# Opening of a fused attention and gated-FFN kernel on one core: weight loads on a second queue, reordered token loads, clearings on other engines, split first products

## The chip, the cores and the metric

The kernel runs on one core of a Trainium2 chip. The metric is device time of one execution in microseconds (us); lower is better. The kernel before has a median of 558.58 us in 3 runs (558.48 to 558.62).

## The reference

One block of a transformer over 2048 tokens of width 576, in bf16:

```
xn = layernorm(x)                                   # x: 2048 x 576
q, k, v = split(xn @ wqkv)                          # 32 heads of width 18
p = softmax(q k^T / sqrt(18)), causal, window 256
s = (p v) @ wo
h = sigmoid(xn @ w_gate) * (xn @ w_up)              # width 4608
g = silu(h @ w_down)
out = x + s * g
```

## The kernel before, in words

The tokens are worked off in four chunks of 512. For each chunk the kernel normalises four tiles of 128 tokens, brings them into the transposed form `xn` (features on the partitions), makes twelve projections (q, k and v for four tiles each), then runs the gate and up products (L910) with the score products (L697) and the products with v (L754) strewn among them, the output projection (L824) and the down projection (L1057, L1088, L1112). TensorE (PE) works with two 64-row halves side by side, so that nearly every product is a pair of matmuls that run together.

Nothing of the order is left to the hardware. Python objects of class `Op` carry an engine, a planned duration, dependencies and a priority; `schedule` (L1158) places them one after the other on five engine lists by planned times, `emit` (L1301) writes the lists out with semaphore waits. Each engine then works its list strictly in order. `deps` become waits on the chip, `odeps` and `behind` only set the order in the plan. The priority counts 40 ns a step, lower first; `slack` is added to the planned arrival of a DMA. So a change of a priority, a slack or a planned duration can move instructions anywhere in the program.

The change is about the first twenty microseconds, chunk 0:

- `build_init` (L367) clears and fills buffers. `pre` fills a tile of ones on VectorE (DVE), `warm` (L394) runs `WARM` = 10 products of 512 columns on it on PE. The identity for the transposes (`id1`, `id2`), masks (`m1`, `m2`, `m3`) and the ones in the v buffer (`vones`, `vpad`) are made on GpSimd (POOL), `hm` on DVE. `pkz` and three `ez` pieces zero the buffers for q and k on ScalarE (ACT): `pkz` the one for tile 0, `ez0` to `ez2` those for tiles 1 to 3.
- `build_ln` (L445) loads a tile of x (`x0` to `x3`, 128 x 576 each, L457), takes the statistics on DVE in two halves (`bn1` L461, `bn2` L463) and joins them (`ag` L465), computes the inverse deviation on POOL (`rstd` L468), applies both on DVE (`apply` L472) and copies 64 columns for the wrap-around (`wrap` L476). In chunk 0 PE transposes the tile in two groups, 8 matmuls that need `apply` and 10 that also need `wrap` (L498), and ACT copies each group from PSUM into `xn` (`xe` L510).
- `build_weights` (L414) loads wqkv: for each of q, k and v four pieces (`load9`, L403), pieces 0 and 3 of 64 x 5 x 288 and pieces 1 and 2 of 64 x 4 x 288.
- `project` (L517) makes one projection: 9 steps of two matmuls (64 rows, 288 columns, L524). For the q products of the tiles named in `Q_SPLIT` it is cut in two: a first part of 8 matmuls, which needs pieces 0 and 1 of the q weights and the first `xe`, and a second of 10, which needs the rest. `build_qk` (L568) brings the result from PSUM into the q and k buffer on ACT and DVE (L586).

In the program before, the DMA queue of SyncE (SP) issues x0, x1, x2, x3, then the four q pieces, four v pieces, four k pieces, then the gate and up weights. ACT issues no DMA. PE's order in the opening is: warm-up, transposes of tiles 0 and 1, first part of q0, transposes of tile 2, first part of q1, second part of q0, transposes of tile 3, second part of q1, then the other products without a break.

Of the kernel before, what the change touches and what calls it, by code (L numbers as in the profile page):

```python
# [8 lines left out]
D = 576  # L9
H = 32  # L10
DH = 18
F = 4608
P = 128
CH = 512
NCH = S // CH
QPC = CH // P
# [8 lines left out]
DP = NKT * P  # L25
# [16 lines left out]
NOT = 4  # L42
# [58 lines left out]
LATE_SLACK = 5000.0  # L101
LN_STEP = 1
EZ = 2
XT_CUT = 4
Q_SPLIT = (0, 1)
# [4 lines left out]
WARM = 10  # L110
X0_SLACK = -250.0
QKV_SLACK = 300.0
X_PRIO = (-9, -9, -9, -9)
# [4 lines left out]
X0_FACTOR = 1.7  # L118
# [100 lines left out]
class Builder:  # L219
# [46 lines left out]
    def alloc_memory(self):  # L266
        nc = self.nc
        bf16, f32 = dt.bfloat16, dt.float32
# [41 lines left out]
        self.pkf = self.pk.bitcast(f32)  # L310
        self.far = self.hT[:, FAR:FAR + 7, :].rearrange("p t c -> p (t c)")[:, 0:NC * FG * P].rearrange(
# [55 lines left out]
    def build_init(self):  # L367
        op = self.op
        self.op_negh = op("DVE", 60, lambda e: e.memset(self.neghalf[:, :], -0.5), "neghalf", prio=0)
        ep = op("POOL", 60, lambda e: e.memset(self.bnst[:, :, 12:14], 0.0), "eps0", prio=-5)  # L370
        self.op_eps = op("POOL", 60, lambda e: e.memset(self.bnst[:, :, 14:15], EPS * D), "eps1", deps=[ep], prio=-5)
        self.op_pre = op("DVE", 250, lambda e: e.memset(self.hT[:, 0, :], 1.0), "pre", prio=-9)
# [11 lines left out]
        h0 = op("DVE", 70, lambda e: e.memset(self.hm[:, :], 0.0), "hm", prio=0)  # L384
        self.op_hm = [op("DVE", 70, lambda e, q=q: e.memset(self.hm[32 * q:32 * q + 32, q % 2:q % 2 + 1], 1.0),
                         f"hm:{q}", deps=[h0], prio=0) for q in range(4)]
        vo1 = op("POOL", 1100, lambda e: e.memset(self.vau[:, :, :, 0:H // 2, DH:DH + 1], 1.0), "vones", prio=1, odeps=[m1])
        self.op_vones = op("POOL", 300, lambda e: e.memset(self.vau[:, :, :, H // 2, :], 1.0), "vpad", deps=[vo1], prio=1)
        self.warm(WARM, "warm:0", [self.op_pre])
        self.op_pkz = [op("ACT", 1300 + 950, lambda e: e.memzero(self.pk[:, 0:2, :, :]), "pkz", prio=0)]  # L390
        self.op_ez = [op("ACT", 930, lambda e, k=k: e.memzero(self.expr[:, 2 * k:2 * k + 2, :, :]), f"ez{k}", prio=0)
                      for k in range(QPC - 1)]
# [21 lines left out]
    def build_weights(self):  # L414
        wq = self.wqkv
        self.op_wqkv = [None] * 3
        for j in range(3):
# [27 lines left out]
    def build_ln(self, c):  # L445
        op = self.op
        pr = 0 if c == 0 else 2
        _, dxn = self.r_xn.take()
        self.op_xn = [[] for _ in range(QPC)]
        for i in range(QPC):  # L450
            st = c * QPC + i
            if c == 0:
                pr = LN_STEP * (i - QPC)
# [3 lines left out]
            o_x = self.dma(xs, self.x[st * P:(st + 1) * P, :], (X0_FACTOR if c == 0 and i > 1 else 1.0) * P * D * 2, f"x{st}",  # L457
                           ("x", i if c == 0 else sx), deps=dx + ([self.op_f1[(c - 1, 6 + 3 * i)]] if c > 0 else []),
                           prio=X_PRIO[i] if c == 0 else 4, slack=X0_SLACK if c == 0 else LATE_SLACK)
# [6 lines left out]
                    f"ag:{st}", deps=[b1, b2, self.op_eps], prio=pr)  # L466
# [9 lines left out]
            wr = op("DVE", 100, lambda e, sr=sr: e.tensor_copy(self.xnr[:, sr, D:DP], self.xnr[:, sr, 0:64]),  # L476
                    f"wrap:{st}", deps=[ap], prio=pr)
# [35 lines left out]
        if c == 0:  # L513
            for o in self.op_ez[EZ:]:
                o.odeps += self.op_xn[-1]
# [907 lines left out]
```

## Time and profile before

| | |
|---|---|
| median of 3 runs | 558.58 us |
| the profiled execution | 558.37 us |
| its span (first to last instruction) | 556.6 us |
| PE busy | 551.4 us, 99% of the span |
| VectorE (DVE) busy | 313.7 us, 56% |
| ScalarE (ACT) busy | 279.8 us, 50% |
| GpSimd (POOL) busy | 31.6 us, 6% |

The profile comes from one execution; times in it count from the start of its span. The profiled execution is 1.77 us longer than its span, and 0.21 us shorter than the median of the runs. In a row of the timeline the first number is the start, the second the length from the first start to the last end of the instructions merged in the row, then engine, source line, operation, tiles and shape, the count, and in brackets the idle time of the engine before it and what ended it. PEld is the weight load of PE, which runs beside its matmuls. "SPq" is the DMA queue that SyncE issues on. Matmuls overlap each other, so the distance from one start to the next says more than the length of one.

### The profile page before, as it was taken

The page shows a single profiled execution, that of the slowest core. Times are in us where ns is not written, and L with a number is a line of the kernel's source. Part 1 is how long each engine was busy: PE and PEld are TensorE (multiplying, and loading weights), DVE is VectorE, ACT ScalarE, POOL GpSimd, SP SyncE. Part 2 cuts the span into 40 slices and gives each one's busy share as a digit, 9 for nine tenths or more (in the row PEclk, how much of TensorE's full clock was granted, in tenths as well). Part 3 has the DMA queues.
Part 4 walks back from the last instruction along what each step waited for, and adds up shares of the span by engine and source line. Part 5 has one row for each costly group of instructions (what it writes and reads, how often), then busy time and mean ns, then how long its engine had stood idle before and what let it go on. Part 6 is the DMA issues. An engine that isn't in the chain of part 4 may idle for free.

```text
span 556.6 us, 18762 instructions
## 1 busy us (share of the span) xinstructions
PE 551.4 (99%) x8144; PEld 307.7 (55%) x8146; DVE 313.7 (56%) x906; ACT 279.8 (50%) x395; POOL 31.6 (6%) x58
## 2 busy tenths in 40 slices
PE   8999999999999999999999999999999999999998
PEld 5755555567555455556755555545665554554554
DVE  5436998515067988633407798853430785885011
ACT  7436886124076757602408678740330875873031
POOL 3000110100000100010000011001000000000100
PEclk9999999999999999999999999999999999999999
DMA  8999979736956666224994766423369465651001
GB/s 203 221 198 207 215 199 241 203 61 121 210 121 141 142 152 139 60 54 63 137 220 113 152 146 149 104 58 69 73 120 223 103 130 130 145 127 32 21 24 42
DMA packets 125929, 73.35 MB, mean 132 GB/s; under 512 B 54680, under 2 KB 125336, under 8 KB 125848
## 3 DMA queue, kind: packets, MB, share of 16 engines
q1 hardware_dynamic: 125848, 72.16, 60.3%
q8 instruction: 64, 1.05, 0.8%
q14 instruction: 17, 0.14, 0.1%
HBM read 55.48 MB, written 2.36 MB: 104 GB/s over the span
## 4 chain that ended last, share of the span: by engine, by line
PE 98%; DMA 0%; DVE 0%; ACT 0%; issue 0%; SPq 0%
PE ps L910 50%; PE ps L1057 22%; PE ps L524 10%; PE ps L697 6%; PE ps L754 4%; PE ps L824 3%; PE ps L1112 2%; PE ps L1088 2%; DMA xr<-in_A_x_dram 0%; ACT xn L510 0%; PE ps L498 0%; SPq L259 0%; DVE bnst L461 0%; DVE xnr L472 0%; DVE mv L465 0%
## 5 line engine op out<-in xcount | busy, mean ns | idle before, releaser
L910 PE MATMUL ps<-xn,wgs 64*128 64x512 bf16 x2522 | 299.1, 376 | 0.0
L910 PEld LDWEIGHTS ps<-xn,wgs 64*128 64x128 bf16 x2522 | 120.4, 94 | 114.8 <-issue 1.1
L712 ACT ACTIVATE expr<-ps 128x1024 bf16<-128x1024 f32 (+1 forms) x152 | 151.1, 1020 | 25.1 <-PE ps L697 24.8
L928 DVE SCALAR_TENSOR_TENSOR hT<-tring,ps 128x512 bf16<-128x512 bf16 x144 | 98.3, 682 | 53.0 <-PE ps L910 33.5
L924 ACT ACTIVATE tring<-ps 128x512 bf16<-128x512 f32 x144 | 86.5, 601 | 80.9 <-PE ps L910 61.5
L1057 PE MATMUL ps<-wd_sb,hT 64*128 64x512 bf16 (+1 forms) x2016 | 125.5, 283 | 0.0
L1057 PEld LDWEIGHTS ps<-wd_sb,hT 64*128 64x128 bf16 x2016 | 64.6, 94 | 59.7
L726 DVE TENSOR_TENSOR expr<-expr,m 128x256 bf16<-128x256 bf16 (+1 forms) x272 | 60.9, 266 | 8.7 <-ACT expr L712 8.0
L697 PE MATMUL ps<-qkp,kd 64*128 64x320 bf16 (+4 forms) x720 | 56.5, 252 | 0.0
L524 PE MATMUL ps<-wqkv_sb,xn 64*128 64x288 bf16 x864 | 54.4, 283 | 0.3 <-ACT xn L510 0.3
L697 PEld LDWEIGHTS ps<-qkp,kd 64*128 64x128 bf16 x720 | 34.0, 94 | 33.8 <-issue 1.0
L680 DVE TENSOR_SCALAR kd<-qkp,hm 128x256 bf16<-128x256 bf16 x176 | 40.2, 289 | 15.2 <-DMA qkp<-pk 13.2
L1146 ACT ACTIVATE expr<-ps 128x576 bf16<-128x576 f32 (+2 forms) x17 | 9.8, 620 | 77.2 <-PE ps L1057 61.8
L524 PEld LDWEIGHTS ps<-wqkv_sb,xn 64*128 64x128 bf16 x864 | 43.0, 94 | 9.6 <-issue 0.3
L1148 DVE SCALAR_TENSOR_TENSOR expr<-expr,ps 128x576 bf16<-128x576 bf16 x12 | 8.5, 751 | 66.3 <-ACT expr L1146 66.3
L849 ACT ACTIVATE sat<-ps 128x576 bf16<-128x576 f32 x16 | 9.5, 648 | 64.9 <-PE ps L824 64.8
L1150 DVE TENSOR_TENSOR expr<-expr,sat 128x576 bf16<-128x576 bf16 (+2 forms) x17 | 7.2, 436 | 43.6 <-ACT expr L1146 34.4
L770 DVE STREAM_TRANSPOSE pk<-ps 128x512 f32<-128x512 f32 x32 | 21.3, 695 | 17.3 <-PE ps L754 17.3
L736 POOL COPY qkp<-qkp 128x256 bf16<-128x256 bf16 x24 | 12.3, 512 | 261.2 <-DVE kd L680 261.2
L787 DVE STREAM_TRANSPOSE op__63<-pk 128x512 bf16<-128x512 bf16 x32 | 22.3, 702 | 0.1
L754 PEld LDWEIGHTS ps<-expr,vau 64*32 64x32 bf16 x1440 | 18.1, 92 | 7.4 <-issue 6.4
L754 PE MATMUL ps<-expr,vau 64*32 64x320 bf16 (+4 forms) x1440 | 20.8, 254 | 0.0
(55 smaller groups left out, 223.6 us busy)
## 6 DMA issues: line engine op xcount, KB each, us to landing
wgs<-in_B_w_gate_dram SPq DMA_DIRECT2D x47, 240.0 KB, 3.8
wgs<-in_B_w_up_dram SPq DMA_DIRECT2D x47, 240.0 KB, 4.8
wgs<-in_B_w_up_dram SPq DMA_DIRECT2D x47, 192.0 KB, 4.1
wgs<-in_B_w_gate_dram SPq DMA_DIRECT2D x47, 192.0 KB, 4.5
wd_sb<-in_B_w_down_dram SPq DMA_DIRECT2D x9, 576.0 KB, 5.5
xf<-in_A_x_dram SPq DMA_DIRECT2D x18, 144.0 KB, 2.8
out_dram<-xf SPq DMA_DIRECT2D x15, 144.0 KB, 4.4
xr<-in_A_x_dram SPq DMA_DIRECT2D x14, 144.0 KB, 4.2
```

What stands on the lines that cost most here:

```text
L524: r = e.matmul(self.bank(ps, HV, hf), self.xn[r0:r0 + 64, k, i * P:(i + 1) * P], self.wqkv_sb[r0:r0 + 64, j, k, :], start=(k == 0), stop=( ...
L680: return e.tensor_scalar(dst, src, self.hm[:, half:half + 1], None, ALU.mult)
L697: i = e.matmul(self.bank(ps, 512, r)[:, pos * 64:(pos + n) * 64], w, self.qkp[r0:r0 + 64, hg, q0 * 64:(q0 + n) * 64], start=True, stop=Tru ...
L712: return e.activation(self.expr[:, es, :, 0:ncol], src, ACTF.Exp, scale=SM_SCALE)
L726: return e.tensor_tensor(ap, ap, m, ALU.mult)
L754: r = e.matmul(self.bank(ps2[s_])[32 * cg:32 * cg + 32, q0 * 64:(q0 + n) * 64], vf[:, v0:v0 + 32], self.expr[p0:p0 + 64, es, cg % 2, pos * ...
L770: tr = self.rd("DVE", dve_ns(CH), lambda e, tf=tf, s_=s_: e.transpose(tf, self.bank(ps2[s_])), f"t1:{c}:{t}", deps=[o, self.op_mul[c][t - ...
L787: t2 = self.op("DVE", dve_ns(CH), lambda e, on=on: e.transpose(self.op_[:, hg % NOT, :], on.rearrange("p g d -> p (g d)")), f"t2:{c}:{hg}" ...
L910: return e.matmul(self.bank((pg, pu)[gu][ft]), w, self.xn[r0:r0 + 64, i, :], start=first, stop=last, tile_position=(r0, 0))
L924: return e.activation(self.tring[:, st_, :], self.bank(ps), ACTF.Tanh, scale=0.5)
L928: return e.scalar_tensor_tensor(self.hT[:, ft, :], self.tring[:, st_, :], 1.0, self.bank(ps), ALU.add, ALU.mult)
L1057: r = e.matmul(self.ps[:, b + n0:b + n1], self.hT[r0:r0 + 64, ft, i * P:(i + 1) * P], self.wd_sb[r0:r0 + 64, q, ft % WDG, n0:n1], start=(s ...
```

## The change

- **Loads.** Pieces 1 and 3 of the q weights are issued from ACT's queue, at the head of ACT's list; they wait for `id1` on POOL (`Q_ACT`). On SP the order becomes x0, x1, q piece 0, x2, q piece 2, x3, then v, k and the rest as before. `X_PRIO`, `Q_PRIO` and the slacks set this.
- **Clearings.** `pkz` stays on ACT, behind the two issues; `ez0` goes to DVE (between `pre` and the first statistics), `ez1` to POOL ahead of the first `rstd`, `ez2` to POOL behind the fourth `rstd`, and with it `m1`, `vones`, `vpad` and then the three `m2`. `neghalf` goes from DVE to POOL, the five `hm` fills on DVE move from the head of the list to behind the evictions of q0 and q1.
- **Split.** The q products of tiles 2 and 3 are split like those of tiles 0 and 1.
- **Warm-up.** 8 products in place of 10.
- **Order that follows from it.** DVE: the statistics of a tile are now joined before those of the next one begin, and the list reads `bn1 bn2 ag` of tile 0, `bn1 bn2` of tile 1, `apply` 0, `ag` 1, `wrap` 0, `bn1 bn2` of tile 2, `apply` 1, `ag` 2, `wrap` 1, `bn1 bn2` of tile 3, `apply` 2, `ag` 3, `wrap` 2, the DVE half of the q0 eviction, `apply` 3, `wrap` 3. PE: transposes of tile 0, first part of q0, transposes of tile 1, second part of q0, first part of q1, transposes of tile 2, second part of q1, first part of q2, transposes of tile 3, second part of q2, first part of q3, then v0, v1 and so on; the second part of q3 comes late among the others. From the gate and up products of chunk 0 on, PE's list differs from before in about a dozen places, where a few score products trade places with gate and up products.
- `m3` on DVE now stands between the evictions of v0 and of v1 and waits for the third `m2` on POOL.

```diff
-EZ = 2
-Q_SPLIT = (0, 1)
+Q_SPLIT = (0, 1, 2, 3)
-WARM = 10
-X0_SLACK = -250.0
+WARM = 8
+X0_SLACK = (-250.0, -400.0, -1000.0, -1200.0)
+Q_SLACK = -200.0
-X_PRIO = (-9, -9, -9, -9)
+X_PRIO = (-20, -19, -17, -15)
+Q_PRIO = (-18, -18, -16, -17)
+Q_ACT = (1, 3)
+AG_PRIO = 0
+WRAP_ENG = "DVE"
+WRAP_NS = 100
+X_EXTRA = (1.0, 1.0, 1.3, 1.3)
-X0_FACTOR = 1.7
...
+        self.expf = self.expr.bitcast(f32)
...
-        self.op_negh = op("DVE", 60, lambda e: e.memset(self.neghalf[:, :], -0.5), "neghalf", prio=0)
+        self.op_pre = op("DVE", 450, lambda e: e.memset(self.hT[:, 0, :], 1.0), "pre", prio=-9)
+        ez = [op(eng, 1100, lambda e, k=k: e.memset(self.expf[:, 2 * k:2 * k + 2, :, :], 0.0), f"ez{k}", prio=p)
+              for k, (eng, p) in enumerate((("DVE", -8), ("POOL", 0), ("POOL", 0)))]
+        self.op_ez = ez
+        self.op_negh = op("POOL", 60, lambda e: e.memset(self.neghalf[:, :], -0.5), "neghalf", prio=-5)
...
-        self.op_pre = op("DVE", 250, lambda e: e.memset(self.hT[:, 0, :], 1.0), "pre", prio=-9)
-        id1 = op("POOL", 200, lambda e: e.memset(self.op_[:, NOT - 1, 0:P], 1.0), "id1", prio=0)
+        id1 = self.op_id1 = op("POOL", 200, lambda e: e.memset(self.op_[:, NOT - 1, 0:P], 1.0), "id1", prio=-6)
...
-            base=0, channel_multiplier=-1), "id2", deps=[id1], prio=0)
+            base=0, channel_multiplier=-1), "id2", deps=[id1], prio=-4)
+        ez[1].odeps.append(self.op_ident)
+        self.op_late = [ez[2]]
         m1 = op("POOL", 300, lambda e: e.memset(self.m64[:, :, :], 1.0), "m1", prio=0)
+        self.op_late.append(m1)
...
-                fill=0.0, base=-(k % 2), channel_multiplier=1 if k == 1 else -1), f"m2:{k}", deps=[m1], prio=0)
+                fill=0.0, base=-(k % 2), channel_multiplier=1 if k == 1 else -1), f"m2:{k}", deps=[m1], prio=3)
...
-        h0 = op("DVE", 70, lambda e: e.memset(self.hm[:, :], 0.0), "hm", prio=0)
+        h0 = op("DVE", 70, lambda e: e.memset(self.hm[:, :], 0.0), "hm", prio=4)
...
+        self.op_late += [vo1, h0]
         self.warm(WARM, "warm:0", [self.op_pre])
-        self.op_pkz = [op("ACT", 1300 + 950, lambda e: e.memzero(self.pk[:, 0:2, :, :]), "pkz", prio=0)]
-        self.op_ez = [op("ACT", 930, lambda e, k=k: e.memzero(self.expr[:, 2 * k:2 * k + 2, :, :]), f"ez{k}", prio=0)
-                      for k in range(QPC - 1)]
+        self.op_pkz = [op("ACT", 1300 + 950, lambda e: e.memzero(self.pk[:, 0:2, :, :]), "pkz", prio=-30)]
...
-            for o in self.op_wqkv[j]:
-                o.slack = QKV_SLACK
+            for k, o in enumerate(self.op_wqkv[j]):
+                o.slack = QKV_SLACK if j else Q_SLACK
+                if j == 0:
+                    o.prio = Q_PRIO[k]
+                    if k in Q_ACT:
+                        o.eng = "ACT"
+                        o.add_dep(self.op_id1)
+                        pkz.behind.append(o)
...
-            o_x = self.dma(xs, self.x[st * P:(st + 1) * P, :], (X0_FACTOR if c == 0 and i > 1 else 1.0) * P * D * 2, f"x{st}",
+            o_x = self.dma(xs, self.x[st * P:(st + 1) * P, :], (X_EXTRA[i] if c == 0 else 1.0) * P * D * 2, f"x{st}",
...
-                           prio=X_PRIO[i] if c == 0 else 4, slack=X0_SLACK if c == 0 else LATE_SLACK)
+                           prio=X_PRIO[i] if c == 0 else 4, slack=X0_SLACK[i] if c == 0 else LATE_SLACK)
...
             if st == QPC - 1:
                 self.op_mask[0].odeps.append(wr)
+                for o in self.op_late:
+                    o.odeps.append(rs)
...
-        if c == 0:
-            for o in self.op_ez[EZ:]:
-                o.odeps += self.op_xn[-1]
```

More of the change, by code (lines that the diff above doesn't have):

```diff
@@ L380, in build_init @@
                 self.m64[0:64, k, :], self.m64[0:64, k, :], pattern=[[-1 if k == 1 else 1, 64]], compare_op=ALU.is_ge,
-                fill=0.0, base=-(k % 2), channel_multiplier=1 if k == 1 else -1), f"m2:{k}", deps=[m1], prio=0)
+                fill=0.0, base=-(k % 2), channel_multiplier=1 if k == 1 else -1), f"m2:{k}", deps=[m1], prio=3)
         self.op_mask = [op("DVE", 130, lambda e: e.tensor_copy(self.m64[64:P, :, :], self.m64[0:64, :, :]), "m3", deps=[m1],
                            prio=2)]
-        h0 = op("DVE", 70, lambda e: e.memset(self.hm[:, :], 0.0), "hm", prio=0)
+        h0 = op("DVE", 70, lambda e: e.memset(self.hm[:, :], 0.0), "hm", prio=4)
         self.op_hm = [op("DVE", 70, lambda e, q=q: e.memset(self.hm[32 * q:32 * q + 32, q % 2:q % 2 + 1], 1.0),
-                         f"hm:{q}", deps=[h0], prio=0) for q in range(4)]
-        vo1 = op("POOL", 1100, lambda e: e.memset(self.vau[:, :, :, 0:H // 2, DH:DH + 1], 1.0), "vones", prio=1, odeps=[m1])
+                         f"hm:{q}", deps=[h0], prio=4) for q in range(4)]
+        vo1 = op("POOL", 1100, lambda e: e.memset(self.vau[:, :, :, 0:H // 2, DH:DH + 1], 1.0), "vones", prio=1)
         self.op_vones = op("POOL", 300, lambda e: e.memset(self.vau[:, :, :, H // 2, :], 1.0), "vpad", deps=[vo1], prio=1)
+        self.op_late += [vo1, h0]
         self.warm(WARM, "warm:0", [self.op_pre])
-        self.op_pkz = [op("ACT", 1300 + 950, lambda e: e.memzero(self.pk[:, 0:2, :, :]), "pkz", prio=0)]
-        self.op_ez = [op("ACT", 930, lambda e, k=k: e.memzero(self.expr[:, 2 * k:2 * k + 2, :, :]), f"ez{k}", prio=0)
-                      for k in range(QPC - 1)]
+        self.op_pkz = [op("ACT", 1300 + 950, lambda e: e.memzero(self.pk[:, 0:2, :, :]), "pkz", prio=-30)]
     def warm(self, n, name, deps):
@@ L475, in build_ln @@
             ring.release(sx, ap)
-            wr = op("DVE", 100, lambda e, sr=sr: e.tensor_copy(self.xnr[:, sr, D:DP], self.xnr[:, sr, 0:64]),
+            wr = op(WRAP_ENG if c == 0 else "DVE", WRAP_NS if c == 0 else 100, lambda e, sr=sr: e.tensor_copy(self.xnr[:, sr, D:DP], self.xnr[:, sr, 0:64]),
                     f"wrap:{st}", deps=[ap], prio=pr)
```

3 lines of the change are left out of this document (2 added, 1 removed).

## The prediction

> **What bounds the kernel now.** First the page (busy times, then the chain that ended last, by engine), then PE's list of waits.
>
> ```profile
> PE 551.4 (99%) x8144; PEld 307.7 (55%) x8146; DVE 313.7 (56%) x906; ACT 279.8 (50%) x395; POOL 31.6 (6%) x58
> PE 98%; DMA 0%; DVE 0%; ACT 0%; issue 0%; SPq 0%
> ```
> ```profile
> PE ps L399 <- DVE hm L384: 1.5, 1, 1.5
> PE ps L498 <- DVE xnr L472: 0.6, 1, 0.6
> PE ps L524 <- ACT xn L510: 0.3, 1, 0.3
> PE ps L1088 <- issue: 0.2, 1, 0.2
> ```
>
> PE is the chain, and it waits four times in all: 1.5 us before the warm-up, 0.6 before the first transpose, 0.3 before the first projection, 0.2 near the end. From the first projection on it runs without a break. So the change can act in one way only: by the moment at which PE has finished the opening and goes over to the gate and up products. Everything behind that moment shifts with it. The chain of waits over the first 30 us gives that moment (columns: start, length, what).
>
> ```profile
> 1.26 2.64 DMA xr<-in_A_x_dram
> 5.77 0.31 PE ps L498 x8
> 6.10 1.20 ACT xn L510 x2
> 7.35 0.67 PE ps L524 x8
> 8.01 0.49 PE ps L498 x18
> 9.97 11.65 PE ps L524 x190
> 21.62 8.40 PE ps L910 x77
> ```
>
> The mark is 21.62. Before it stand 216 projection matmuls (108 pairs) and 72 transposes (4 groups of 18). A pair costs 11.65 / 95 = 0.1226 us, so four pairs (a first part) 0.49 and five (a second part) 0.61; a transpose group costs 0.46 to 0.49, I take 0.46. What lies in front of PE is DVE's list:
>
> ```profile
> 3.05 0.46 DVE L461 BATCH_NORM_STATS2 bnst<-xr 128x6 f32<-128x288 bf16 x1 [1.08 <-DMA xr<-in_A_x_dram]
> 3.43 0.44 DVE L463 BATCH_NORM_STATS2 bnst<-xr 128x6 f32<-128x288 bf16 x1
> 3.93 0.46 DVE L461 BATCH_NORM_STATS2 bnst<-xr 128x6 f32<-128x288 bf16 x1
> 4.30 0.20 DVE L465 BATCH_NORM_AGGREGATE mv<-bnst 128x2 f32<-128x15 f32 x1
> 4.59 0.57 POOL L468 TENSOR_TENSOR rstd<-mv,neghalf 128x1 f32<-128x1 f32 x1 [0.82 <-DVE mv L465]
> 5.22 0.41 DVE L472 TENSOR_SCALAR xnr<-xr,mv,rstd 128x576 bf16<-128x576 bf16 x1
> ...
> 6.63 0.45 DVE L461 BATCH_NORM_STATS2 bnst<-xf 128x6 f32<-128x288 bf16 x1
> 7.00 0.45 DVE L463 BATCH_NORM_STATS2 bnst<-xf 128x6 f32<-128x288 bf16 x1
> 7.40 0.43 DVE L472 TENSOR_SCALAR xnr<-xf,mv,rstd 128x576 bf16<-128x576 bf16 x1
> ...
> 7.87 0.17 DVE L476 COPY xnr<-xnr 128x64 bf16<-128x64 bf16 x1
> ```
>
> The reader is to see two things. The `ag` of tile 0 starts at 4.30 though its second statistics end at 3.87, because the first statistics of tile 1 stand before it. And the lower rows (with `ag` between the last two) are just the order that the changed list repeats for each tile (`bn1 bn2 apply ag wrap`): from `bn1` to `apply` 0.77, from `apply` to the end of `wrap` 0.64.
>
> **Part 1, DVE's order.** With `ag` 0 right behind `bn2` 0 it starts at about 3.90; `rstd` begins 0.29 later and takes 0.57, `apply` follows 0.06 on: 4.82 in place of 5.22, a gain of 0.40, if tile 1 is there in time. For now both `bn` of tile 1 stand before `apply` 0. If x1 lands at L1, `apply` 0 starts at the later of 4.82 and L1 + 0.03 + 0.77. I call that start A.
>
> **Part 2, the loads.** Landings before, from the loads' rows (the number at the end: issue to landing), and the rate at which the DMAs moved data:
>
> ```profile
> L259 SPq DMA_DIRECT2D xr<-in_A_x_dram x2: 395/406/417, 0.8 to 1.3; - x2
> DMA to landing us min/median/max: 2.2/2.4/2.6
> ```
> ```profile
> DMA to landing us min/median/max: 2.8/2.8/2.8
> ```
> ```profile
> 1.72 0.91 SPq L259 DMA_DIRECT2D xf<-in_A_x_dram  x2
> ```
> ```profile
> L259 SPq DMA_DIRECT2D wqkv_sb<-in_A_wqkv_dram x2: 614/684/754, 2.7 to 3.5; - x2
> DMA to landing us min/median/max: 3.7/3.9/4.0
> ```
> ```profile
> wqkv_sb<-in_A_wqkv_dram SPq DMA_DIRECT2D x6, 180.0 KB, 4.1
> wqkv_sb<-in_A_wqkv_dram SPq DMA_DIRECT2D x6, 144.0 KB, 3.9
> ```
> ```profile
> 1.80:4.00 2.20, 2.20 (x6) 0.76 (x5) 1.01 (x5) 2.19 (x3) 1.78 (x5) 1.00 0.88 251
> ```
>
> (The single landing row is that of x2 and x3; the last number of the last row is GB/s.) So x0 landed at 3.0, x1 at 3.87, x2 at 4.52, q piece 1 at 3.46 + 3.7 = 7.16. That piece, and not the ACT copy that the wait names, held the first projection at 7.35: the copy it needs had ended at about 6.7. In the changed kernel piece 1 is issued about 2.4 us sooner (ACT waits only for `id1`), and piece 0 0.95 us sooner (1.72 for 2.67), so both should land before 6.5. The price is paid by x: the queues share one stream of 251 GB/s that starts near 1.8. A tile of x and a small q piece are 147 KB, 0.59 us each; a large q piece 184 KB.
>
> - L1: 3.87 if nothing of piece 1 comes ahead of x1, 3.87 + 0.59 = 4.46 if all of it does. I take the middle, 4.16.
> - L2: ahead of x2 on SP stand x0, x1, piece 0, with itself 627 KB, done at 1.8 + 2.50 = 4.30; before, x2's 442 KB were through at 3.56 and it landed 0.96 later, so 5.26 at best. With pieces 1 and 3 ahead as well, 958 KB, 6.58. I take 5.92.
> - L3 (issued about 3.65): at best 3.65 + 2.8 = 6.45; with everything ahead, 1254 KB, 7.75. I take 7.4.
>
> The page "DMA: Bandwidth & Descriptors" of the Trainium skill (Issuing engines are not separate DMA queues) speaks against this part: DMAs of all engines run on the same 16 DMA engines and interleave, and a second issuing engine only saves issue time. By that rule the late ends hold, as in the second rival; no run here shows two queues at once yet.
>
> **Part 3, the split and PE's order.** The first transposes come at A + 0.55 (5.22 to 5.77 before), their copy on ACT 0.33 later (5.77 to 6.10), and it takes 0.60:
>
> ```profile
> L510 ACT ACTIVATE xn<-ps 128x512 bf16<-128x512 bf16 x4 | 2.4, 597 | 1.1 <-PE ps L498 1.1
> ```
>
> With 0.05 to PE, the first part of q0 starts at A + 1.53. After that PE has, if nothing stalls: 0.49, transposes 0.46, second part 0.61, first part 0.49 (A + 3.58), transposes 0.46, 0.61, 0.49, transposes 0.46, 0.61 (A + 6.21), and then 216 - 54 = 162 matmuls, 81 pairs, 9.93: the mark is at A + 16.14. Before, from 5.22, it was 16.40; the split and the earlier weights are worth 0.26. A split itself adds no matmul.
>
> The stalls: `apply` 1 stands behind both `bn` of tile 2, so the transposes of tile 1 wait until L2 + 0.03 + 0.77 + 0.55 = L2 + 1.35, and those of tile 2 likewise until L3 + 1.35. Before, `apply` 1 stood at 6.07 with tile 2 long there; this is the new wait, and behind it on DVE stand `ag` 2, `wrap` 1 and all of tile 3, and PE waits for them.
>
> Sum with the values taken: A = 4.16 + 0.80 = 4.96; PE is through the first part of q0 at 6.98; tile 1 is ready at 5.92 + 1.35 = 7.27, stall 0.29; tile 2 at 7.4 + 1.35 = 8.75, where PE comes at 4.96 + 3.58 + 0.29 = 8.83, no stall. Mark: 4.96 + 16.14 + 0.29 = 21.39, that is **0.23 sooner**. Early end (L1 up to 4.02, L2 up to 5.49, L3 up to 7.05): A = 4.82, mark 20.96, 0.66 sooner. Late end (4.46, 6.58, 7.75): A = 5.26, tile 1 at 7.93 for 7.28, stall 0.65, mark 22.05, 0.43 later.
>
> **Part 4, clearings and issues.** All cost nothing, for these covers:
>
> ```profile
> 0.80 1.28 ACT L390 ACT_TABLE_LOAD   x1 [0.80 <-PEq L1408]
> ...
> 0.98 0.48 DVE L372 MEMSET hT<- 128x512 bf16 x1 [0.98 <-PEq L1408]
> ...
> 2.10 1.06 ACT L390 ACTIVATE pk<-pk 128x1024 uint32<-128x1024 uint32 x1
> ```
> ```profile
> L353 POOL MEMSET pk<- x4: 1805/1805/1806, 106.4 to 515.7; 128x2048 bf16 x4
> ```
>
> ACT issues two pieces from about 1.1 (0.75 and 0.62 by the SP rows), loads its table (1.28) and clears `pk` (1.06; the three `ez` pieces that followed it are gone from ACT): done near 4.9, and its first copy is due at A + 0.88 = 5.8. `ez0` on DVE: a fill of 512 columns there took 0.48, so 1024 about 1.0, from 1.5 to 2.5; the statistics start at 3.05. Both are idle time. `ez1` on POOL: half of 1.81, 0.9, over before `rstd` 0 is due at 4.2. `ez2`, `m1`, `vones`, `vpad` and `m2` come behind `rstd` 3 (about 9.8): 0.9 for `ez2` and, as an estimate from the small fills, some 2.5 for the others, until about 13.2. The first v product ends near 12.8 and its evictions, which need the ones, near 13.7; then comes `m3`. If POOL were later than that, `m3` would hold the evictions of v1 and with them a pair of PSUM banks; PE has four pairs, so up to one projection (9 pairs, 1.1 us) of lateness is covered, and beyond that it costs what it exceeds. The `hm` fills move into DVE's idle time between evictions.
>
> **Part 5, the warm-up.** PE's weight loads in the warm-up show when it ran at which pace.
>
> ```profile
> 1.52 3.67 PE L399 MATMUL ps<-hT 128*128 128x512 bf16 x10 [1.52 <-DVE hm L384]
> ...
> 4.06 0.15 PEld L399 LDWEIGHTS ps<-hT 128*128 128x128 bf16 x1 [0.28 <-issue]
> ...
> 4.38 0.31 PEld L399 LDWEIGHTS ps<-hT 128*128 128x128 bf16 x2 [0.17 <-issue]
> ```
>
> The first seven products start at 1.52 to 4.06, 0.42 apart; then the distance drops, and the last two take 0.8 with their tails. So PE worked at half pace for about 2.7 us and was let off near 4.2, at the seventh product. Eight are enough by this one execution, with one to spare; the ninth and tenth end nothing. I take 0. Afterwards PE idles from about 4.8 to 5.5 in place of 5.19 to 5.77.
>
> The page "TensorE: Matmul & The Clock Gate" of the Trainium skill (Part 1: The HAM clock gate) says that PE runs at half clock until a window of about 3.4 us is busy, that this window runs free of the kernel's start, and that an idle window throttles again. By that the pause of under 1 us is harmless, but eight products, 3.4 us when all are slow, can end before a late window does; the trace neither bears this out nor excludes it, having one phase only.
>
> **Part 6, the rest of the list.** In about a dozen places score products and gate and up products trade places. PE has 0.2 us of idle time behind the opening, so little can be won; a swap that leaves PE waiting for one exponential of 1024 columns costs at most about 1.0 us, by the ACT rows above (1.06 for 1024 columns). Nothing in the list points to one: 0, between -0.2 and +1.0.
>
> **The sum.** Against the profiled execution 558.37 - 0.23 = 558.14; the median of the runs lies 0.21 above it, so **558.35** for the median. The parts' ends without rivals: 558.58 - 0.66 - 0.2 = 557.7 and 558.58 + 0.43 = 559.0.
>
> **The rivals.**
> 1. *PE falls into half pace* (the other side). The eight products end before PE is let off, or the thin stretch until 7 us puts it back. Then the opening's products run at half pace until another 2.7 us of work is done, and since PE has gaps there and transposes are short, for some 4 us of work: half of it, 1.35 to 2, is lost. For it: two products fewer, more pause. Against it: let off at the seventh. 558.35 + 1.8 = **560.2**. It decides if the release comes later than about 4.9. Chance 0.11.
> 2. *x pays for q*: x2 and x3 land past the late end because two queues of small pieces move less than 251 GB/s; at 210 x2 lands at 1.8 + 4.56 + 0.96 = 7.3, x1 near 4.8, A = 5.6, tile 1 at 8.65 for 7.62, mark 22.8, 1.2 later: 559.8; half of the way there is likelier, **559.3**. For it: eight loads issued by 4 us in place of six, four of them in small pieces. Against it: the middle values already count most of the bytes. Chance 0.12, a quarter of it past +0.2%.
> 3. *The pieces on ACT come no sooner*: ACT issues late or its queue is served after SP's. Then q0 starts at 7.35 as before, with the new list behind it: 7.35 + 14.61 = 21.96, **558.9**. Against it: nothing stands on ACT before them but `id1`. Chance 0.05.
> 4. *The later list stalls* (part 6): **559.2**. Chance 0.05. *It gains*, with the early end of the opening, over 1.1 us in all: **557.4**. Against it: 0.2 of idle time. Chance 0.04.
>
> **How the numbers follow.** The forecast has the remaining 0.63, with a time of 558.35 and its own range 557.7 to 559.0. 0.2% of 558.58 is 1.12 us, about what a measurement of this kernel can tell from no change. Faster by that: rival 4's second half, 0.04, and 0.01 of the forecast's edge, 0.05. Slower: rival 1 (0.11), a quarter of rival 2 (0.03), a trace of rival 4, 0.15. Within: 0.80. Range: 557.6 to 559.5 leaves out rival 1, the far part of rival 2 and the gain, not quite 0.2.
>
> **What would show it.** In the changed profile: `ag` 0 ahead of `bn1` 1 and `apply` 0 at 4.8 to 5.3 (part 1); x1 at 3.9 to 4.5, x2 at 5.3 to 6.6, q piece 1 before 6 (part 2); the first part of q0 at 6.4 to 6.8 and a gap on PE of 0 to 0.7 ahead of tile 1's transposes (part 3); the first gate and up product at 21.0 to 22.0. Projection pairs more than 0.2 apart would be rival 1. The prediction is wrong if the mark moves by more than 1 us, or if PE shows new waits behind it.

## The result, and the profile after

| | before | after |
|---|---|---|
| median of 6 runs each, us | 558.53 (558.17 to 558.62) | 561.36 (560.93 to 562.75) |
| ratio, 95% interval | | 1.0055 (1.0043 to 1.0068) |
| profiled execution, us | 558.37 | 560.93 |
| its span, us | 556.6 | 559.1 |
| first gate and up product (the mark) | 21.62 | 24.20 |

The changed kernel is 2.8 us, 0.55%, slower: outside the range of the prediction. One execution of the kernel before and one of `a_w10late` (an experiment below) took three to six times as long as all others of the same kernel; both are left out. The place is the one that the prediction watches. From the mark to the end of the span it is 534.9 us in the kernel after and 535.0 before, so in these two executions nothing behind the opening counts, neither the places where products trade places nor anything else. All that follows is about the first 24 us.

Busy times and the chain by engine, from the page of the kernel after:

```profile
PE 553.0 (99%) x8142; PEld 307.9 (55%) x8144; DVE 314.9 (56%) x906; ACT 277.6 (50%) x392; POOL 32.7 (6%) x61
PE 98%; DMA 1%; DVE 1%; SPq 0%; issue 0%; ACT 0%; DVEq 0%
```

PE's list of waits, kernel after (what waited, for what, total, times, longest):

```profile
PE ps L410 <- DVE hT L375: 1.5, 1, 1.5
PE ps L541 <- ACT xn L530: 1.0, 1, 1.0
PE ps L518 <- DVE mv L483: 0.5, 1, 0.5
PE ps L518 <- DVE xnr L490: 0.4, 1, 0.4
PE ps L1105 <- issue: 0.2, 1, 0.2
```

PE is busy 1.6 us longer with two products fewer, and it waits 1.0 us more. Both say where to look: waits in the opening, and products that take longer. The chain of waits over the first 30 us, kernel after:

```profile
2.53 5.05 DMA xf<-in_A_x_dram
...
8.42 0.34 DVE xnr L490
...
8.80 0.66 PE ps L518 x18
9.47 1.22 PE ps L541 x10
...
11.16 1.82 DVE xnr L490
12.97 0.05 issue
13.02 0.59 PE ps L518 x18
13.61 10.58 PE ps L541 x172
24.20 5.81 PE ps L927 x53
```

Before, the chain left DMA at 3.90 and DVE before 5.77. Now the load of x2 holds it until 7.58, and `apply` of tile 3 (L490) again from 11.16 to 12.97. The timeline of the kernel after shows the rows behind it:

```profile
1.52 3.60 PE L410 MATMUL ps<-hT 128*128 128x512 bf16 x8 [1.52 <-DVE hT L375]
...
5.05 0.41 DVE L490 TENSOR_SCALAR xnr<-xr,mv,rstd 128x576 bf16<-128x576 bf16 x1
...
7.25 1.15 PE L541 MATMUL ps<-wqkv_sb,xn 64*128 64x288 bf16 x8 [0.98 <-ACT xn L530]
7.60 0.46 DVE L479 BATCH_NORM_STATS2 bnst<-xf 128x6 f32<-128x288 bf16 x1 [1.92 <-DMA xf<-in_A_x_dram]
...
9.28 2.03 PE L541 MATMUL ps<-wqkv_sb,xn 64*128 64x288 bf16 x18
...
10.78 0.95 POOL L376 MEMSET expr<- 128x1024 f32 x1
...
11.16 1.81 DVE L490 TENSOR_SCALAR xnr<-xf,mv,rstd 128x576 bf16<-128x576 bf16 x1
...
11.67 0.26 POOL L388 MEMSET m<- 128x192 bf16 x1
11.86 0.94 POOL L399 MEMSET vau<- 128x192 bf16 x1
```

Three things are to be seen. **L, the loads:** tile 2 begins at 7.60, after 1.92 us of idle DVE; 5.92 was taken for its landing and 6.58 as the late end. **C, the clock of PE:** the first eight projection products take 1.15 us (0.67 before, in the chain); they start 0.24 us a pair apart for 0.12, and that goes on until 10.7. The eight warm-up products (3.60 us) had been 0.42 apart to their end, so in this execution PE never came to full pace before 10.7. **P, the fills on POOL:** the same `apply` that took 0.41 at 5.05 takes 1.81 at 11.16, and ends 0.17 us after the third of three fills that follow each other on POOL (11.86 + 0.94 = 12.80).

The landings (issue to landing, us, at the end) come from the groups by tile, first x2 and x3, then the q piece 0 alone, kernel after:

```profile
L264 SPq DMA_DIRECT2D xf<-in_A_x_dram x2: 603/714/824, 2.5 to 4.1; - x2
...
DMA to landing us min/median/max: 4.8/4.9/5.0
```
```profile
L264 SPq DMA_DIRECT2D wqkv_sb<-in_A_wqkv_dram x1: 762/762/762, 1.7 to 1.7; - x1
DMA to landing us min/median/max: 5.4/5.4/5.4
```

x2 and x3 took 2.8 before, q piece 0 about 4. Piece 0 landed at 1.72 + 5.4 = 7.1, which is what the first projection at 7.25 waited for (the wait names an ACT copy; the one that these products need ran from 6.04 for 0.60 and had ended at 6.64). And the DMAs moved no more than before. Busy times by stretch, kernel after; the last number is GB/s, the one ahead of the last two the granted clock:

```profile
1.80:4.00 2.20, 2.20 (x6) 0.76 (x5) 1.56 (x3) 1.53 (x2) 0.55 (x1) 1.00 0.91 244
4.00:9.00 5.00, 3.12 (x37) 1.40 (x35) 2.99 (x12) 2.00 (x3) 1.16 (x3) 1.00 1.12 230
```

244 and 230 GB/s, against 251 in the first stretch before: two issuing engines, one stream. (The granted clock reads 1.00 here though the pairs are 0.24 apart, as it does in the first stretch before, where the warm-up products are 0.42 apart: the half pace that a run starts with is not in this record. A later fall is, as the experiments show.)

### The profile page after: what moved, and what is told of

Its sections match the earlier page's. It is cut to its first block, busy times and chain, and to the rows that moved or that the text cites. A ratio compares the mean times of both kernels' runs of the same rounds, so it can differ in the third digit from the quotient of the medians.

```text
span 559.1 us, 18756 instructions
## 1 busy us (share of the span) xinstructions
PE 553.0 (99%) x8142; PEld 307.9 (55%) x8144; DVE 314.9 (56%) x906; ACT 277.6 (50%) x392; POOL 32.7 (6%) x61
## 4 chain that ended last, share of the span: by engine, by line
PE 98%; DMA 1%; DVE 1%; SPq 0%; issue 0%; ACT 0%; DVEq 0%
PE ps L927 50%; PE ps L1074 22%; PE ps L541 9%; PE ps L714 6%; PE ps L771 4%; PE ps L841 3%; PE ps L1129 2%; PE ps L1105 2%; DMA xf<-in_A_x_dram 1%; DVE xnr L490 0%; SPq L264 0%; PE ps L518 0%; DVE bnst L481 0%; ACT expr L1163 0%; DVE expr L1167 0%
## 5 line engine op out<-in xcount | busy, mean ns | idle before, releaser
L541 PE MATMUL ps<-wqkv_sb,xn 64*128 64x288 bf16 x864 | 56.0, 286 | 1.0 <-ACT xn L530 1.0
```

What stands on the lines that cost most here:

```text
L541: r = e.matmul(self.bank(ps, HV, hf), self.xn[r0:r0 + 64, k, i * P:(i + 1) * P], self.wqkv_sb[r0:r0 + 64, j, k, :], start=(k == 0), stop=( ...
```

## The experiments

Additional warm-up products and fillers write a PSUM bank that nobody reads. The engine lists are those of the kernel that is edited, but for the edit. "Mark" is the first gate and up product in the profiled execution (for `a_w10late` that is the one left out, so it has none).

| kernel | median us (range, runs) | ratio to before, 95% | mark |
|---|---|---|---|
| `b_act`: before, q pieces 1 and 3 on ACT | 560.86 (560.64 to 561.33, 5) | 1.0042 (1.0029 to 1.0054) | 23.87 |
| `b_w8`: before, 8 warm-ups | 558.46 (558.10 to 559.58, 11) | 1.0005 (0.9996 to 1.0014) | 21.48 |
| `a_w12`: after, 12 warm-ups | 562.24 (561.10 to 563.09, 5) | 1.0066 (1.0054 to 1.0078) | 26.32 |
| `a_late`: after, POOL fills late | 561.43 (559.88 to 562.23, 6) | 1.0053 (1.0039 to 1.0066) | 24.07 |
| `a_w12late`: both | 559.89 (559.44 to 561.33, 7) | 1.0027 (1.0017 to 1.0038) | 22.70 |
| `a_w10late`: late fills, 10 warm-ups | 560.90 (559.41 to 561.14, 4) | 1.0036 (1.0023 to 1.0050) | |
| `a_fill_late`: late fills, 4 fillers | 559.71 (559.50 to 562.64, 11) | 1.0027 (1.0018 to 1.0037) | 22.90 |
| `a_xswap`: after, x2 and x3 early | 561.53 (560.44 to 562.52, 5) | 1.0056 (1.0044 to 1.0068) | 24.55 |
| `a_w10late_onesp`: `a_w10late`, loads on SP | 559.69 (558.96 to 560.27, 11) | 1.0018 (1.0010 to 1.0027) | 23.51 |
| `a_loads0`: after, old loads | 560.14 (559.00 to 560.84, 11) | 1.0024 (1.0015 to 1.0033) | 24.12 |
| `a_3undone`: old loads, late fills, 12 | 559.38 (559.20 to 559.96, 11) | 1.0017 (1.0008 to 1.0025) | 22.63 |
| `a_3undone_w10`: the same with 10 | 559.19 (559.00 to 560.68, 11) | 1.0015 (1.0006 to 1.0024) | 22.45 |

### The second queue alone: `b_act`

The kernel before with nothing but the two issues moved.

```diff
+        first = [o for o in prog["SP"] if o.name in ("wqkv0.1", "wqkv0.3")]
+        prog["SP"][:] = [o for o in prog["SP"] if o not in first]
+        for o in first:
+            o.eng = "ACT"
+            o.add_dep(self.op_id1)
+        prog["ACT"][:0] = first
```

> The kernel before with q pieces 1 and 3 taken from SP's list and issued at the head of ACT's, all else as it was. Theory L (two queues at once only share the same stream, and every landing gets later): x2 and x3 later by 0.6 to 1.5, the first projection at 7.5 to 8.5 for 7.35, 0.3 to 1.3 slower, 558.9 to 559.8. Theory N (the second queue is harmless, only the order of x behind q hurts): 558.2 to 558.7.

Measured: 2.3 us slower, nearly as much as the whole change. The rows of x2 and x3, the first projection, and two stretches of `b_act`:

```profile
DMA to landing us min/median/max: 4.1/4.8/5.6
```
```profile
6.83 1.38 PE L498 MATMUL ps<-op__63,xnr 64*128 64x64 bf16 x36 [1.48 <-DVE xnr L472]
...
8.57 1.14 PE L524 MATMUL ps<-wqkv_sb,xn 64*128 64x288 bf16 x8 [0.36 <-DMA wqkv_sb<-in_A_wqkv_dram]
```
```profile
8.00:10.00 2.00, 1.64 (x36) 1.12 (x32) 1.32 (x6) 1.47 (x4) 0.88 (x2) 0.50 1.19 229
...
12.00:14.00 2.00, 2.00 (x48) 1.71 (x42) 0.91 (x2) 1.94 (x5) 0.00 (x0) 1.00 1.16 235
```

x2 and x3, ahead of every q piece on SP, land 4.1 and 5.6 us after issue for 2.8, because the pieces on ACT now come between. In the old order of DVE the first statistics of tile 2 stand ahead of `apply` 0, so PE stands still 1.48 us ahead of the first transposes, and later it falls back to half pace: the granted clock reads 0.50 and the eight products take 1.14, in spite of ten warm-ups. So the expectation had the direction and not the size: late loads cost once as a wait and once more through the clock. The edit changes two things at once, the queue of the two pieces and their place in the stream, now ahead of x2 and x3; a run with both pieces ahead of x2 on SP alone, which would part the two, was not made.

### Fewer warm-ups alone: `b_w8`

```diff
-            for k in range(n):
+            for k in range(8 if not isinstance(e, Counter) else n):
```

(The planner still counts ten, so that no list moves; `a_w12` and its kin do the same the other way round.)

> The kernel before with 8 warm-up products in place of 10, all lists else as they are. Theory C: half pace reaches into the projections in some or all runs, 1 to 2 slower than before, 559.5 to 560.5, with a larger spread. Theories L and P: within 0.2 of 558.5.

Measured: no difference (1.0005, with 1 inside the interval), but five of eleven runs lie above 558.9, where those of the kernel before lie below 558.8. The profiled one, at 558.24, ran its warm-up at half pace to the end (8 products in 3.60 us) and still is at full pace from its first projection:

```profile
6.84 0.67 PE L524 MATMUL ps<-wqkv_sb,xn 64*128 64x288 bf16 x8
```

With the old order and loads, eight products cost nothing in six of eleven runs and 0.4 to 1.1 us in five, of which no trace was kept. So the number of warm-ups alone does not explain the 2.8 us.

### More warm-ups, later fills, and both

`a_w12` is the line above with 12 for 8 in the kernel after. `a_late` lets the fills on POOL wait for `wrap` of tile 3, so that they run beside none of the four `apply`:

```diff
                 for o in self.op_late:
                     o.odeps.append(rs)
+                    if o.eng == "POOL":
+                        o.add_dep(wr)
```

> The changed kernel with 12 warm-up products in place of 8, all lists else as they are. Theory C (half pace: eight products end before PE is let off, so 13 projection pairs from 7.25 to 10.7 cost 0.24 in place of 0.12): pairs at 0.12 from the first projection on, the first gate and up product about 1.0 to 1.8 sooner, 559.6 to 560.4, and the runs closer together. Theory L (the late load of x2 holds the opening, and the half pace only fills time that PE would wait anyway): within 0.4 of 561.4. Theory P (DVE's last apply, 1.8 long beside POOL's fills, holds the opening): within 0.4 of 561.4.

> The changed kernel with a wait in front of POOL's late fills (the third ez piece, masks, ones of v): they start after the wrap of tile 3 in place of after its rstd, so they no longer run beside DVE's last apply. Theory P: that apply takes 0.43 again in place of 1.81, PE's wait of 0.44 ahead of the transposes of tile 3 goes, 0.4 to 0.8 faster than the changed kernel, 560.6 to 561.0. Theories C and L: within 0.3 of 561.4, and the apply may still be long if POOL's fills are not the cause.

> The changed kernel with 12 warm-up products and with POOL's late fills behind the wrap of tile 3: half pace and the long apply undone together. Theory H (they hide each other: whichever is left ends at the same moment, so undoing one gave nothing): pairs at 0.12, no wait ahead of the transposes of tile 3, first gate and up product near 22.9 in place of 24.2, 559.9 to 560.3; what is left over the kernel before, 1.3, is the late x2. Rival: they are both beside the point and the late loads hold everything: 561.2 to 561.6. A stall of PE without a cause shown, as in the kernel with 12 products alone (1.66), may come on top.

Measured: neither alone gains anything (562.24 and 561.43 for 561.36), and `a_w12` lies above all that was expected of it; both together gain 1.5 us. The rows say why. `a_w12`, timeline:

```profile
7.28 0.67 PE L541 MATMUL ps<-wqkv_sb,xn 64*128 64x288 bf16 x8 [0.64 <-DMA wqkv_sb<-in_A_wqkv_dram]
...
11.12 2.03 DVE L490 TENSOR_SCALAR xnr<-xf,mv,rstd 128x576 bf16<-128x576 bf16 x1 [0.29 <-POOL rstd L486]
...
12.05 0.94 POOL L399 MEMSET vau<- 128x192 bf16 x1
...
13.21 0.59 PE L518 MATMUL ps<-op__63,xnr 64*128 64x64 bf16 x18 [1.13 <-DVE xnr L490]
```

Twelve warm-ups put PE at full pace, but then it stands 1.13 us before the transposes of tile 3, since `apply` 3 is held until 13.15, 0.16 us after the end of `vones` (L399; 0.17 in the kernel after). `a_late`, timeline, chain and one stretch:

```profile
8.78 2.34 PE L543 MATMUL ps<-wqkv_sb,xn 64*128 64x288 bf16 x18
...
10.64 0.42 DVE L490 TENSOR_SCALAR xnr<-xf,mv,rstd 128x576 bf16<-128x576 bf16 x1
```
```profile
8.41 0.55 PE ps L520 x18
...
24.07 6.02 PE ps L929 x55
```
```profile
10.00:12.00 2.00, 2.00 (x34) 1.48 (x32) 0.98 (x3) 1.04 (x3) 1.14 (x2) 0.50 1.15 268
```

Late fills give `apply` 3 its 0.42 back, but PE is at half pace and comes late to tile 3 anyway. Each of the two covers the other. In `a_w12late` both are gone (chain):

```profile
8.48 0.54 PE ps L520 x18
...
22.70 7.32 PE ps L929 x67
```

One thing in `a_w12` stays open. Its profiled execution, at 563.09 the slowest of the five, has a pause of 1.66 us amid the projections, from 19.34 to 21.0, for which the trace names no releaser ("issue"). An instruction fetch starts between 18 and 19; the kernel before has one between 20 and 20.5 and no pause, and what the cause is was not tried. Without the pause that execution would lie at 561.4. Two other runs of `a_w12` were at 561.1 and 561.5, so the reading of the pair does not hang on it; the last two, at 562.24 and 562.64, have no trace.

### Is it the clock? Ten warm-ups, and fillers in the pause

`a_w10late` has the late fills and ten warm-ups. `a_fill_late` has the late fills and eight, and puts four products of 512 columns between the transposes of tile 0 and the first projection, where PE waits anyway:

```diff
+        pe = prog["PE"]
+        at = next(k for k, o in enumerate(pe) if o.name == "qk:0:0:0:0")
+
+        def f_fill(e):
+            for k in range(4):
+                r = e.matmul(self.ps[:, 3 * 512:4 * 512], self.hT[:, 0, 0:P], self.hT[:, 0, :], start=True, stop=True)
+            return r
+        pe.insert(at, Op("PE", 4 * WARM_NS, f_fill, "fill", [], 0))
```

> The changed kernel with 10 warm-up products and the late fills behind the wrap of tile 3. Theory C (a thin window in front of the first projections brings PE back to half pace or keeps it there, depending on the phase of a run): between the kernel with late fills alone (561.4) and the one with 12 products and late fills (559.9), spread over 1 us or more, median 560.0 to 561.0. Theory W (only the number of warm-up products counts, ten are enough as in the kernel before): 559.3 to 559.8, spread under 0.5.

> The changed kernel with the late fills behind the wrap of tile 3, 8 warm-up products, and 4 more such products in PE's pause between the transposes of tile 0 and the first projection. Theory C: they keep PE busy in that window, so the pace holds or comes sooner: 559.6 to 560.6, against 561.43 for late fills alone. If the window does not matter: 561.2 to 562 (the four products can put the first projection off by up to 0.5).

Measured: ten leave it at 560.9 (with one run at 559.41), fillers bring 559.71, 1.7 us less than `a_late`, although they add work and tile 1 came later (8.69 for 8.41). `a_fill_late`, timeline, chain and the stretch that was shown of `a_late`:

```profile
6.09 1.41 PE L1320 MATMUL ps<-hT 128*128 128x512 bf16 x4
7.43 0.66 PE L543 MATMUL ps<-wqkv_sb,xn 64*128 64x288 bf16 x8
```
```profile
8.69 0.54 PE ps L520 x18
...
22.90 7.10 PE ps L929 x65
```
```profile
10.00:12.00 2.00, 2.00 (x61) 1.66 (x59) 1.60 (x8) 2.00 (x5) 0.99 (x2) 1.00 1.18 238
```

61 products in the two microseconds for 34, at a granted clock of 1.00 for 0.50. The lack of two products is not enough to explain it, since ten lose the pace as well; more work in front of the projections keeps it in most runs, four products in the pause or four more in the warm-up (`a_w12late`, 559.89). In `a_late` the first eight projection products (6.87, 0.67 us) had still run at full pace; the fall came only after them, with no single pause over 1.0 us before it.

The mean granted clock of each run says the same without any edit. `b_act`, `a_late`, `a_xswap` and `a_loads0` have one fall in their traces, to 0.50, from 8.00, 8.81, 9.26 and 9.10 us on and for 3.4 us each; such a run has a mean of 0.997. Where runs of one kernel differ in it, those at 0.997 are slower than those at 1.000: 560.85 to 561.14 against 559.41 in `a_w10late`, 560.35 to 560.84 against 559.00 to 560.14 in `a_loads0`, 561.33 against 559.44 to 560.19 in `a_w12late`, 560.68 against 559.00 to 559.45 in `a_3undone_w10`. By the medians one fall costs 1.2 to 1.5 us. All runs of the kernel before are at 1.000, four of the six of the kernel after below it (0.997 or 0.994). Not every slow run is explained: two of `a_late` (561.94, 562.23) and one of `a_fill_late` (562.64) are at 1.000 and have no trace.

The page "TensorE: Matmul & The Clock Gate" of the Trainium skill (Part 1: The HAM clock gate) says that the pace goes by how busy a free-running window of about 3.4 us was. The falls of 3.4 us and the effect of the fillers agree with that. The same page of the Trainium skill (Why this matters for your kernels) asks only that no gap between bursts is over some 3 us; here pauses of 1.0 and 0.9 us, in a stretch with little work, were enough, and the measurement decides.

### The loads: `a_xswap`, `a_w10late_onesp`, `a_loads0`

`a_xswap` keeps both queues and puts x2 and x3 behind x1 on SP. `a_loads0` issues the first eight loads from SP in the order of before; `a_w10late_onesp` is `a_w10late` ("the first kernel" in its expectation) with the eight on SP as x0, x1, q0, q1, x2, q2, q3, x3. The second edit below is that of `a_loads0`; `a_w10late_onesp` has the same with its own order of names.

```diff
+        sp = prog["SP"]
+        xs = [o for o in sp if o.name in ("x2", "x3")]
+        sp[:] = [o for o in sp if o not in xs]
+        sp[2:2] = xs
```
```diff
+        names = ["x0", "x1", "x2", "x3", "wqkv0.0", "wqkv0.1", "wqkv0.2", "wqkv0.3"]
+        first = sorted((o for e in ("SP", "ACT") for o in prog[e] if o.name in names), key=lambda o: names.index(o.name))
+        for e in ("SP", "ACT"):
+            prog[e][:] = [o for o in prog[e] if o not in first]
+        for o in first:
+            o.eng = "SP"
+            o.deps = []
+        prog["SP"][:0] = first
```

> The changed kernel with x2 and x3 moved on SP's list right behind x1, ahead of q pieces 0 and 2; ACT still issues pieces 1 and 3. Theory L: x2 lands near 5.5 in place of 7.58, the transposes of tile 1 come near 7.0 in place of 8.80, 1.3 to 2.0 faster, 559.4 to 560.1. Theory C: PE at half pace fills most of that time; what goes is its wait of 0.41 ahead of those transposes, and q piece 0 comes later, so 0 to 0.5 faster, 560.9 to 561.4.

> As the first kernel of this call, but all loads on SP alone, in the order x0, x1, q pieces 0 and 1, x2, q pieces 2 and 3, x3: the new order without a second queue. Theory Q (the second queue makes every landing later): x2, issued near 3.1, lands near 6.1 (for 7.2 to 7.6), piece 1 near 6.3, first projection near 6.8, 0.3 to 1.0 faster than the first kernel of this call. Theory O (the order, x behind q, is what costs): the same as that kernel or slower, x3 issued near 5 and landing near 8 holds tile 2.

> The changed kernel with its first eight loads all on SP in the order of before (x0 to x3, then the four q pieces), warm-up and fills as changed. Theory L with H: x2 lands near 4.5 and the first projection starts near 7.4 (q piece 1), tile 1 is transposed by 8.3, then the half pace or the long apply still costs about 1: first gate and up product 22.8 to 23.6, 559.8 to 560.6. If the loads are everything: 558.5 to 559.0. If they are nothing: 561.4.

Measured: with both queues the order on SP does not help. `a_xswap`, PE's waits:

```profile
PE ps L541 <- DMA wqkv_sb<-in_A_wqkv_dram: 2.3, 1, 2.3
```

x2 and x3 still took 4.5 and 5.1 us, and now q piece 0 came at 8.4, where it held the first projection by 2.30. One queue in place of two, with the order that goes with it, is worth 1.2 us in `a_w10late_onesp` (559.69 for 560.9), 1.2 us also in `a_loads0` against the kernel after. In `a_w10late_onesp` that is about what one fall costs: all its eleven runs are at 1.000, three of the four of `a_w10late` at 0.997. In `a_loads0` x2 lands after 2.9 us, its profiled execution still falls to half pace (0.50 from 10 to 12) and has its mark at 24.12, later than expected, and its runs spread over 1.8 us. So the early issue from ACT costs by itself, as `b_act` has it, and the other two costs are not undone with it.

### All three undone: `a_3undone`, `a_3undone_w10`

Old loads, late fills, and 12 or 10 warm-ups, by the edits above.

> The changed kernel with all three undone: loads as before, 12 warm-up products, late fills behind the wrap of tile 3. What stays of the change is the order on DVE and PE, the split of all four q products and the clearings on DVE and POOL. If these three causes are all: 558.4 to 559.3. If something else is behind it: above 560.

> The changed kernel with the loads of before, late fills, and 10 warm-up products in place of the 12 of the earlier run (559.38), whose warm-up ended at 6.82 and put off the first transposes. If nothing else costs: first projection near 7.2 to 7.4, first gate and up product near 22.1, 558.7 to 559.1. If the changed order itself is thin enough to lose the pace (three pauses): 559.3 to 560.3 with a spread.

Measured: 559.38 and 559.19, both just above what was expected, and 0.8 and 0.6 us above before. PE's waits and the chain of `a_3undone_w10`:

```profile
PE ps L543 <- DMA wqkv_sb<-in_A_wqkv_dram: 1.8, 2, 0.9
```
```profile
8.61 1.28 PE ps L543 x18
...
22.45 7.55 PE ps L929 x70
```

In `a_3undone_w10` the rest is in the order of PE's list. The second part of q0 now stands right behind the transposes of tile 1 and needs q piece 3, which the old loads bring only at about 8.6 (issued at 4.77); PE waits for it 0.94 us. Before, the transposes of tile 2 and the first part of q1 stood ahead of it. That is what the early issue of piece 3 was needed for, and by `b_act` (2.3 us) the early issue costs more than it covers. An order of PE's list without this wait was not tried. In `a_3undone` the chain runs through the twelve warm-up products instead, which end at 6.82.

No run points to a version below the kernel before; `b_w8`, the nearest, cannot be told from it.

## Why the prediction was wrong, point by point

Three steps failed: the landing of x2 (part 2), the fills that were to cost nothing (part 4), and the warm-up that was to cost nothing (part 5).

**The sum.** The forecast's mark was 21.39; it became 24.20, 2.81 later. By the forecast's own terms tile 1 is ready at 7.27 and the mark follows 21.39 - 7.27 = 14.12 later. Measured: 8.80 and 15.40. So 1.53 us are lost ahead of the transposes of tile 1 and 1.28 behind them. The experiments confirm the cut: with C and P gone, the second number is 22.70 - 8.48 = 14.22 (`a_w12late`) and 22.90 - 8.69 = 14.21 (`a_fill_late`), within 0.1 of the forecast, and all that is left is x2's lateness.

**Part 1, right.** `ag` 0 stood ahead of `bn1` 1 and A was 5.05 (4.96 forecast, 4.8 to 5.3 allowed). It bought nothing, since PE then waited for weights.

**Part 2, the first step that failed.** L1 came at 1.26 + 3.0 = 4.26 (4.16 taken), and q piece 1, from ACT, at 1.04 + 3.6 = 4.6. L2 came at 7.58 for 5.92 and for 6.58 at the late end, L3 at 4.05 + 4.8 = 8.9 for 7.4, and q piece 0 at 7.1 where "both land before 6.5". The step counted x2 as half of the way between the pieces on ACT coming all behind it and all ahead, at 251 GB/s. With all of them ahead, 958 KB, and the measured rates of 244 and 230, x2 would be due at 1.8 + 4.03 + 0.96 = 6.8. The other 0.8 us is 181 KB more that the DMAs moved by then, about as much as q piece 2 and a little of x3, both issued behind x2. They still land behind it, piece 2 at 3.39 + 4.9 = 8.3 and x3 at 8.9, so either their bytes move in part ahead of its last ones, or what lies between the last byte and the landing is longer than 0.96; this is worked out from the rates and stays open. The rule that the step weighed, from the page "DMA: Bandwidth & Descriptors" of the Trainium skill (Issuing engines are not separate DMA queues), was the better guide, and the middle value was the wrong choice. It is rival 2, "x pays for q", at about its full price: its mark of 22.8 lies 1.4 behind the forecast's, and 1.53 were measured. Its reason holds only in part, since the DMAs moved 244 and 230 GB/s and not 210.

**Part 3, right in its lengths.** The terms behind tile 1 hold within 0.1, as said. The forecast's stall of 0.29 ahead of tile 1 became the link of the chain, since x2 came late. What it overlooked is the dependence on q piece 3, which with the old loads is worth 0.94 us of waiting.

**Part 4, the step "All cost nothing" failed.** Its covers hold for what waits for the fills: `m3` and the evictions held up nobody. It did not ask what a fill does to an instruction that runs beside it. Three fills in a row behind `rstd` 3 held `apply` 3 for 1.81 us in place of 0.42, 2.03 in `a_w12`; with PE at full pace PE stands 1.13 us for it. At half pace it hides for the most part: the weight load of the next transpose waited 0.44.

**Part 5, "Eight are enough" and "0", half wrong.** For the kernel before it is true in the median (`b_w8`), though "one to spare" is not: that release near 4.2 belongs to one execution. In the changed kernel it is wrong: without the wait of 0.44, half pace would have put PE 1.28 - 0.44 = 0.84 behind at tile 3 in the kernel after, and it cost 24.07 - 8.41 - 14.12 = 1.54 in `a_late`. It is rival 1 with both its clauses. In the profiled execution of the kernel after the eight products ended before PE was let off; in `a_late`, in `b_act` and, by their mean clocks, in four other runs of the kernel after PE was put back. Its price was 1.35 to 2. What went wrong is its chance, 0.11: it was set as if it were independent of rival 2. It is not. Late loads make PE pause, so rival 2 brings rival 1 with it, and `b_act` shows both from one edit. Both rivals together, with their prices (560.2 and 559.3, that is 1.85 and 0.95 over the forecast) added, lie at 558.35 + 1.85 + 0.95 = 561.15, within 0.3 of the measured time.

**Part 6, right.** The rest of the list cost nothing: 534.9 and 535.0.

## What to carry to other kernels

- Where loads already fill the stream, issuing from a second engine only changes which bytes come first; before adding it, sum the bytes ahead of each load that the critical path needs, and take the late end.
- An opening that just reaches the full pace of PE has no spare pause: a load that comes 1 us later can cost its wait and about as much again by the clock (`b_act`: 2.3 us in all), so such rivals are added and not weighed one by one.
- A fill moved to an idle engine can still hold another engine: look at what runs beside it, and undo suspects in pairs, since one cost can cover the other.

## What the runs showed of the hardware that was not expected

- **A chain of fills on POOL holds a bf16 `apply` on DVE to its end.** 128 x 576 bf16, subtract and multiply: 0.41 to 0.43 us alone, 1.81 and 2.03 beside three back-to-back fills, and it ends 0.17 and 0.16 us after the last of them. With the fills behind it (`a_late`) it takes 0.42 again. `a_loads0` and `a_xswap` cannot tell: there it began late in the third fill (ending at 9.80 + 0.94 = 10.74 and 10.55 + 0.94 = 11.49), ended at 10.90 and 11.65, again 0.16 later, and took 0.44 and 0.48, hardly longer than alone. The cast of a projection from PSUM beside the same fill took its usual 0.46.

```profile
10.78 0.46 DVE L603 CAST pk<-ps 128x288 bf16<-128x288 f32 x1 [0.49 <-PE ps L541]
```

  The page "SBUF — State Buffer" of the Trainium skill (Who interferes with whom) states it: `tensor_scalar` in a mode that uses two ports shares a pair of them with GpSimd, the pair is locked for a whole instruction, and the other engine blocks fully. The rows agree and add that DVE did not get in between the three fills either; why it then needed only 0.16 to 0.17 us more, and not its whole 0.42, they do not show.
- **PE falls back to half pace without a long pause.** In `a_late`, pauses of 0.3, 1.0 and 0.9 us between 5 and 8.5 us were enough for a granted clock of 0.50 from 8.8 to 12.2 us.
- **A second issuing engine moved no more bytes, and what stood behind its pieces landed later.** x2 and x3: 2.8 us from issue to landing with one queue before, 4.8 to 5.0 after and 4.1 to 5.6 in `b_act`; x0, ahead of them, 2.2 to 2.3 in all three. From 1.8 to 4.0 us the DMAs moved 251 GB/s before, 244 after and 210 in `b_act`.
